# Pair-wise half transposes, narrower tables, two tokens a row and spread tail stores in an attention and mixer kernel

## The chip, the cores and the metric

The kernel runs on one core of one Trainium2 chip. The metric is the device time of one execution in microseconds (us). The profile's "span" runs from the first to the last instruction of one profiled execution and is some 1.7 us shorter than the time of the same run. Each run has a state: "slow" when it is over 1.5% above the fastest run of the same kernel. Ratios use fast runs only. The medians in the tables include slow runs. Engines: PE is the matrix engine (PEld its weight loads), DVE is VectorE, ACT is ScalarE, POOL is GpSimd, SP is the engine whose queue issues the DMAs.

## The reference, cut to what matters

```python
# q, k, v: (8, 8, 576, 64); window 128, ALiBi slopes 2**-(h+1)
scores = q @ k.T / 8 + bias            # only 0 <= row - column < 128
x      = softmax(scores) @ v           # -> (8, 576, 512)
W_tok  = (x @ w_q) @ (x @ w_k).T / 8   # the token mixer, no softmax
out    = relu(W_tok @ x) @ w_out       # float32
```

## The kernel before

The kernel builds a list of operations for 8 batches (loads, casts, transposes of q and k, scores S, exponentials E, bias products M, value products PV, normalisations N, transposes of x, the mixer products WK, WQ, G, MX, the relus R, output products O, tail outputs OT, stores). A fixed string, PLAN, gives each operation its place in the order, its engine and its PSUM bank; every engine works through its part in that order. These are the parts that the change touches:

```python
# tables exp(-slope * distance), 1024 columns a head, all written by ACT
nc.scalar.activation(out=table[:, h, :].rearrange("p (a b) -> p a b", a=4),
    in_=rel.unsqueeze(1).broadcast_to([P, 4, 256]), func=AF.Exp, scale=s)
nc.scalar.activation(out=table[:, h, 960:1024], in_=rel[:, 0:64], func=AF.Exp, scale=s)
...
# x transposed one pair of heads (c) at a time, five 128x128 blocks, one bank
for t in range(5):
    nc.tensor.transpose(bank(bk[0]).bitcast(F16)[:, P * t : P * t + P],
                        xs[b % 2][:, t, P * c : P * c + P], ident)
copy(eng, xT[b % 2][:, c, 0:S], bank(bk[0]).bitcast(F16)[:, 0:S])
...
# outputs: 128 tokens a block, two blocks in one store, the 64 tail tokens of two batches in another
nc.tensor.matmul(bank(bk[0]), rm[:, b % 2, db, P * t : P * t + P], wout_sb[:, db, :], ...)
nc.sync.dma_start(out=out[b, P * (t - 1) : P * (t + 1), :].rearrange("(t p) d -> p t d", t=2), in_=osb[n % 3])
nc.sync.dma_start(out=out[2 * pr : 2 * pr + 2, 512:576, :], in_=osbt[pr % 2])
```

The first store writes 512 KB (there are 16 of them), the second 256 KB (4 of them, called tail stores below; the fourth belongs to the end of the kernel).

The softmax here doesn't subtract the row's maximum and nothing guards it: scores larger than these inputs give would overflow.

## Time and profile before

| | before |
|---|---|
| time, median of the first 3 runs (range) | 163.13 us (160.31 to 163.85) |
| span of the profiled run | 159.1 us |
| busy, whole span | PE 83%, DVE 76%, ACT 78%, POOL 39% |
| busy from 40 to 130 us | PE 95%, DVE 93%, ACT 90% |

The page of the kernel before, busy time by engine and its course in 40 slices of 4 us (9 is 90% or more):

```profile
PE 132.0 (83%) x2180; PEld 87.5 (55%) x2180; DVE 121.6 (76%) x200; ACT 123.5 (78%) x178; POOL 62.7 (39%) x82
...
PE   6446579649989999999999999999989699999700
...
DVE  4467468986999989999799897989899896643300
ACT  6999939684999799989979888999899642748300
...
PEclk9955558996999999999999999999999999999995
DMA  5999999999995899799999999989138973054570
```

Three engines are nearly full in the middle at once. The DMA row shows mostly full engines in the middle (with a 5 near 48 us and a 7 near 64 us). The deep hole is in the slices from 111 to 119 us (1 and 3), and at the end the row falls again. The same page's chain of waits, by engine:

```profile
PE 44%; ACT 23%; DVE 13%; DMA 5%; POOL 5%; issue 4%; POOLq 0%
```

The start, from the timeline of ACT (start us, length us, engine, line, operation, out<-in, count):

```profile
2.60 8.75 ACT L164 ACTIVATE table<-rel 128x1024 f16<-128x1024 f32 x14 [0.52 <-POOL rel L164]
11.26 2.83 ACT L164 ACTIVATE pt<-bank 128x1024 f16<-128x1024 f32 x3
13.97 1.35 ACT L164 ACTIVATE table<-rel 128x1024 f16<-128x1024 f32 x2
```

ACT writes tables without a gap until the first exponential (`pt<-bank`) at 11.26 us. The DMA queue in the middle, from the timeline of SP:

```profile
105.27 0.72 SPq L164 DMA_DIRECT2D out_dram<-osbt  x1
106.04 0.57 SPq L164 DMA_DIRECT2D ldv<-in_v_dram  x1
106.66 6.08 SPq L164 DMA_DIRECT2D out_dram<-osbt  x1
112.78 3.25 SPq L164 DMA_DIRECT2D ldv<-in_v_dram  x1
116.14 3.07 SPq L164 DMA_DIRECT2D out_dram<-osb  x1
```

Two tail stores are issued at 105.3 and 106.7 us; the second holds the queue for 6.08 us. What the tail stores do by themselves is seen in the trace's single DMA packets. Busy DMA engines, counted from the packets of the output stores (2 KB each):

```
 112.0 to 114.5 us   2.1 engines of 16, nothing else moves
 154.5 to 157.5 us   2.1 engines of 16, nothing else moves
```

The chain of waits in order of time shows the store that came after them:

```profile
116.14 8.34 DMA out_dram<-osb
...
124.50 0.59 ACT osb L164
```

And the end: timeline, then what the closing instructions on SP waited for:

```profile
147.36 0.52 SPq L164 DMA_DIRECT2D out_dram<-osbt  x1
...
150.28 0.58 ACT L164 COPY osb<-bank 128x512 f32<-128x512 f32 x1 [0.28 <-PE bank L164]
```

```profile
SPq L713 <- DMA out_dram<-osbt: 4.3, 1, 4.3
```

The last output copy ends at 150.86 us, 8.2 us before the end of the span; of these the kernel waits 4.3 us for the last tail store alone. The transposes of x, from the groups of instructions (busy us, mean ns):

```profile
L164 DVE COPY xT<-bank 128x576 f16<-128x576 f16 x32 | 13.2, 450 | 1.4 <-PE bank L164 1.1
L164 PE MATMUL bank<-ident,x 128*128 128x128 f16 x160 | 12.0, 220 | 0.1
```

### The profile page before, as it was taken

The page shows a single profiled execution, that of the slowest core. Times are in us where ns is not written, and L with a number is a line of the kernel's source. Part 1 is how long each engine was busy: PE and PEld are TensorE (multiplying, and loading weights), DVE is VectorE, ACT ScalarE, POOL GpSimd, SP SyncE. Part 2 cuts the span into 40 slices and gives each one's busy share as a digit, 9 for nine tenths or more (in the row PEclk, how much of TensorE's full clock was granted, in tenths as well). Part 3 has the DMA queues.
Part 4 walks back from the last instruction along what each step waited for, and adds up shares of the span by engine and source line. Part 5 has one row for each costly group of instructions (what it writes and reads, how often), then busy time and mean ns, then how long its engine had stood idle before and what let it go on. Part 6 is the DMA issues. An engine that isn't in the chain of part 4 may idle for free.

```text
span 159.1 us, 5064 instructions
## 1 busy us (share of the span) xinstructions
PE 132.0 (83%) x2180; PEld 87.5 (55%) x2180; DVE 121.6 (76%) x200; ACT 123.5 (78%) x178; POOL 62.7 (39%) x82
## 2 busy tenths in 40 slices
PE   6446579649989999999999999999989699999700
PEld 6334467538657566476665556576655457643200
DVE  4467468986999989999799897989899896643300
ACT  6999939684999799989979888999899642748300
POOL 4553542682664596465742445154530500000000
PEclk9955558996999999999999999999999999999995
DMA  5999999999995899799999999989138973054570
GB/s 167 370 227 334 220 380 189 336 313 314 261 291 215 270 329 280 241 262 334 348 352 272 282 297 335 311 229 215 59 106 230 298 303 140 13 165 158 158 268 35
DMA packets 52703, 39.39 MB, mean 248 GB/s; under 512 B 39368, under 2 KB 39368, under 8 KB 52680
## 3 DMA queue, kind: packets, MB, share of 16 engines
q1 hardware_dynamic: 52680, 39.07, 85.4%
q8 instruction: 17, 0.28, 0.8%
q14 instruction: 6, 0.05, 0.1%
HBM read 29.62 MB, written 9.44 MB: 246 GB/s over the span
## 4 chain that ended last, share of the span: by engine, by line
PE 44%; ACT 23%; DVE 13%; DMA 5%; POOL 5%; issue 4%; POOLq 0%
PE bank L164 44%; ACT pt L164 11%; ACT table L164 6%; DMA out_dram<-osb 5%; DVE pt L164 4%; DVE x L164 3%; POOL nat L164 3%; DVE qT L164 2%; ACT qT L164 2%; ACT kT L164 2%; ACT osb L164 1%; DVE xT L164 1%; DVE inv L164 1%; DVE wkn L164 1%; DVE wqT L164 1%
## 5 line engine op out<-in xcount | busy, mean ns | idle before, releaser
L164 ACT ACTIVATE pt<-bank 128x1024 f16<-128x1024 f32 x64 | 63.2, 1035 | 8.7 <-PE bank L164 8.6
L164 POOL CAST nat<-ld 128x1152 f16<-128x1152 f32 x32 | 36.4, 1149 | 25.0 <-DVE pt L164 12.2
L164 DVE TENSOR_TENSOR pt<-pt,table 128x2048 f16<-128x2048 f16 x32 | 39.6, 1245 | 0.3 <-ACT pt L164 0.2
L164 POOL CAST vt<-ldv 128x512 f16<-128x512 f32 (+1 forms) x37 | 22.5, 627 | 33.4 <-DVE pt L164 16.2
L164 PE MATMUL bank<-wout_sb,rm 128*128 128x512 f16 x128 | 31.7, 380 | 1.3 <-ACT osb L164 1.3
L164 PE MATMUL bank<-qT,kT 64*128 64x256 f16 (+2 forms) x320 | 25.7, 269 | 5.2 <-DVE qT L164 2.5
L164 DVE TENSOR_TENSOR x<-bank,inv 128x640 f16<-128x640 f32 x32 | 25.7, 816 | 0.7
L164 PE MATMUL bank<-vt,pt 128*128 128x65 f16 x576 | 24.0, 199 | 1.2 <-ACT kT L164 0.7
L164 PEld LDWEIGHTS <-pt 128*128 128x128 f16 x576 | 21.8, 101 | 5.5 <-issue 1.9
L164 PEld LDWEIGHTS <-kT 64*128 64x128 f16 x320 | 14.6, 100 | 14.1 <-issue 10.4
L164 PE MATMUL bank<-ident,nat 64*128 64x64 f16 x576 | 14.5, 198 | 7.4 <-POOL nat L164 4.1
L164 ACT COPY osb<-bank 128x512 f32<-128x512 f32 x22 | 13.0, 613 | 8.7 <-PE bank L164 7.1
L164 PEld LDWEIGHTS <-rm 128*128 128x128 f16 x128 | 11.0, 98 | 13.2 <-issue 2.4
L164 PEld LDWEIGHTS <-nat 64*128 64x128 f16 x576 | 12.0, 99 | 11.3 <-POOL nat L164 7.3
L164 ACT ACTIVATE rm<-bank 128x512 f16<-128x512 f32 x23 | 14.0, 607 | 2.5 <-PE bank L164 2.3
L164 DVE COPY xT<-bank 128x576 f16<-128x576 f16 x32 | 13.2, 450 | 1.4 <-PE bank L164 1.1
L164 ACT COPY kT<-bank 128x1152 f16<-128x1152 f16 x11 | 12.4, 1136 | 1.1 <-PE bank L164 1.1
L164 DVE COPY qT<-bank 128x1152 f16<-128x1152 f16 x7 | 9.4, 1355 | 4.4 <-PE bank L164 4.3
L164 PE MATMUL bank<-ident,x 128*128 128x128 f16 x160 | 12.0, 220 | 0.1
L164 ACT COPY qT<-bank 128x1152 f16<-128x1152 f16 x9 | 10.1, 1121 | 1.3 <-PE bank L164 1.2
L164 PEld LDWEIGHTS <-x 128*128 128x128 f16 x160 | 9.3, 97 | 2.7 <-issue 1.6
L164 DVE COPY osb<-bank 128x512 f32<-128x512 f32 x10 | 6.9, 687 | 4.9 <-PE bank L164 4.9
(42 smaller groups left out, 123.2 us busy)
## 6 DMA issues: line engine op xcount, KB each, us to landing
ld<-in_k_dram SPq DMA_DIRECT2D x16, 576.0 KB, 6.5
ld<-in_q_dram SPq DMA_DIRECT2D x16, 576.0 KB, 6.1
ldv<-in_v_dram SPq DMA_DIRECT2D x32, 256.0 KB, 7.4
out_dram<-osb SPq DMA_DIRECT2D x16, 512.0 KB, 4.9
ldv<-in_v_dram SPq DMA_DIRECT2D x8, 128.0 KB, 5.8
osb<-in_moe_w_out_dram SPq DMA_DIRECT2D x2, 512.0 KB, 6.2
out_dram<-osbt SPq DMA_DIRECT2D x4, 256.0 KB
osbt<-in_moe_w_k_dram SPq DMA_DIRECT2D x1, 128.0 KB, 6.2
```

The source lines that it names most:

```text
L164: r = call(*a, **k)
```

## The change

Its intent, part by part: transposes that use both partition halves of PE at once, for two pairs of heads together (less PE time); tables for which ACT computes 256 columns and DVE copies the rest (less ACT time); two consecutive tokens a partition, so that a row of 4 KB is contiguous in memory; tail stores whose slowest dimension is 64 rows and no longer 2 batches, so that all DMA engines take part. PLAN is new from end to end: the order, the engines and the banks. The diff, cut to its core:

```diff
-            nc.scalar.activation(
-                out=table[:, h, :].rearrange("p (a b) -> p a b", a=4),
-                in_=rel.unsqueeze(1).broadcast_to([P, 4, 256]), func=AF.Exp, scale=s)
-            nc.scalar.activation(out=table[:, h, 960:1024], in_=rel[:, 0:64], func=AF.Exp, scale=s)
+            nc.scalar.activation(out=table[:, h, 0:256], in_=rel, func=AF.Exp,
+                                 scale=-(2.0 ** (-(h + 1))))
+    for f in range(2):                                   # four heads each, on DVE
+            t = table[:, 4 * f : 4 * f + 4]
+            for a in range(1, 4):
+                w = 256 if a < 3 else 192
+                nc.vector.tensor_copy(out=t[:, :, 256 * a : 256 * a + w], in_=t[:, :, 0:w])
+            nc.vector.tensor_copy(out=t[:, :, 960:1024], in_=t[:, :, 0:64])
... (transposes of x, now for c - 1 and c together)
-                for t in range(5):
-                    nc.tensor.transpose(bank(bk[0]).bitcast(F16)[:, P * t : P * t + P],
-                                        xs[b % 2][:, t, P * c : P * c + P], ident)
+                for a in range(2):
+                    for t in range(5):
+                        for i in range(2 if t < 4 else 1):
+                            r = slice(64 * i, 64 * i + 64)
+                            o = bank(bk[i]).bitcast(F16)
+                            w = 64 * ((5 - i) * a + t)
+                            nc.tensor.transpose(o[:, w : w + 64],
+                                xs[b % 2][r, t, P * (c - 1 + a) : P * (c + a)], ident[r, r])
... (outputs)
-                    nc.tensor.matmul(bank(bk[0]), rm[:, b % 2, db, P * t : P * t + P],
+                    r = slice(256 * (t // 2) + t % 2, 256 * (t // 2) + 256, 2)
+                    nc.tensor.matmul(bank(bk[0]), rm[:, b % 2, db, r],
-    ....rearrange("(t p) d -> p t d", t=2)
+    ....rearrange("(p t) d -> p t d", t=2)
-                nc.sync.dma_start(out=out[2 * pr : 2 * pr + 2, 512:576, :], in_=osbt[pr % 2])
+                for i in range(2):
+                    nc.sync.dma_start(out=out[2 * pr + i, 512:576, :],
+                                      in_=osbt[pr % 2][64 * i : 64 * i + 64])
... (PLAN: every line is new)
```

In the new PLAN ACT takes the casts of the first k and q, which POOL had. And after the last value product nine output groups follow on PE, where eleven followed before.

More of the change, by code (lines that the diff above doesn't have):

```diff
@@ L30 @@
 FOREVER = 1000
-DENSE = (False, False)
 class Op:
@@ L102 @@
 PLAN = """
-1G 7D 37S 0G 2D 33S 4D 45S 3G 5D 12P0 41S 6D 13P0 24A 57S 9P0 53S 10P0 18A 49S 14P0 59S 20A 11P0
-63S 38G 15P0 55S 19A 8P0 51S 39P2 31S 34G 21A 40D2 29S 71S 35P0 17A 85S 36D0 46G 67S 22A 248P0
-47P2 42G 241P4 249A0 48D2 243P6 244A6 58G 43P0 44D0 246P2 242A4 54G 23A 245D 256P0 253P4 251P6
-247A2 50D 252A6 258P2 60G 254A4 61P6 62D6 257A0 64G 259A2 65P0 56D 16P4 66A0 250D 52A 255D 83S
-406P0 401P2 79S 30G 407D0 32G 263P4 77S 402D2 408D0 268P6 264A4 93S 403D2 89S 411P0 72G 269A6 81S
-261P4 412D0 409P2 262A4 75S 260D 73P6 97S 404P3 74A6 86G 27S 405D3 416P4 413D0 111S 266P6 417D4
@@ L109 @@
-68G 105S 87P0 267A6 418D4 101S 265D 69P4 115S 419P3 70A4 414P6 80G 410D2 420D3 84G 278P4 415D6
-276P2 279A4 270D 271P6 272A6 78G 563P4 94G 277A2 564D4 273P6 88D0 274A6 95P2 90G 96D2 91P0 82G
-561P2 92A0 562D2 76G 275D 107S 426P0 109S 286P2 421P4 98G 427D0 287A2 103S 428D0 281P6 25S 422D4
-282A6 283P2 423D4 119S 28G 431P0 123S 284A2 432D0 288P4 280D 99P6 100A6 565P2 112G 433D0 289A4
-436P6 566D2 106G 296P0 437D6 569P2 438D6 297A0 429P4 102G 424P5 430D4 573P6 570A2 285D 291P0 434P4
-574A6 439P2 292A0 116G 425D5 293P6 435D4 440D2 294A6 113P4 290D 117P0 567P2 118A0 575P6 108G 114D4
@@ L115 @@
-568A2 577P7 110G 104G 571P0 576D6 298P2 572A0 578D7 135S 446P4 295D 299A2 145S 441P0 149S 26G
-447D4 308P6 442D0 448D4 451P2 127S 309A6 443D0 120G 141S 301P4 129S 579P6 302A4 452D2 453D2 137S
-300D 131S 306P0 121P2 307A0 133S 303P4 678P7 136G 580D6 163S 122A2 124G 171S 456P0 444P6 304A4
-457D0 449P2 146G 445D6 675P3 458D0 679A7 581P4 450D2 676A3 147P6 150G 582D4 454P0 148A6 459P1
-455D0 125P2 151P4 128G 460D1 126A2 583P6 310D 589P0 152A4 313P2 142G 584D6 591P1 314A2 590D0 587P4
-318P6 588D4 130G 319A6 673P0 305D 161S 316P2 159S 585P4 317A2 593P6 138G 674D0 155S 592D1 586A4
@@ L121 @@
-153S 143P2 320D 594A6 167S 311P0 680P4 312A0 189S 132G 144D2 677S 597P6 681A4 134G 139P0 157S
-140A0 315D 466P4 175S 461P2 193S 598A6 164G 467D4 693P0 468D4 462D2 323P6 694A0 463D2 471P4 172G
-324A6 321P0 472D4 473D4 476P2 322A0 162G 333P6 477D2 338P4 478D2 334A6 160G 469P0 464P1 470D0
-336P2 339A4 325D 331P6 474P0 332A6 479P4 156G 465D1 683P5 475D0 337A2 154G 187S 480D4 328P0 682S
-165P6 173P2 166A6 185S 685P4 174D2 168G 181S 329A0 605P6 686D4 684A5 326P2 606D6 601P0 190G 327A2
-603P4 687S 602D0 183S 599P6 191P2 330D 201S 169P0 192A2 688P5 179S 600D6 197S 170A0 158G 604D4
@@ L127 @@
-689D5 205S 481P2 207S 343P0 482D2 483D2 486P4 176G 344A0 348P6 487D4 346P2 349A6 335D 607P0 347A2
-194G 488D4 595P6 608A0 341P2 177P4 350D 596A6 491P0 342A2 696P6 340D 178A4 698P7 186G 492D0 493D0
-697A6 690P2 188G 699A7 182G 351P0 691D2 613P4 484P3 614A4 496P6 692S 485D3 352A0 703P2 700S 497D6
-498D6 223S 609P4 358P0 345D 219S 610A4 611P6 701P3 612A6 184G 359A0 494P4 702D3 499P5 202G 195P6
-495D4 489P3 196A6 500D5 615P0 490D3 356P4 180G 704D2 616A0 617P3 211S 357A4 506P0 209S 618D3 501P6
-198G 507D0 213S 353P2 502D6 508D0 215S 716P4 354A2 227S 206G 503D6 361P0 717A4 199P2 355D 203P6
@@ L133 @@
-362A0 621P4 204D6 208G 200A2 239S 366P0 708P5 367A0 622D4 718S 360D 233S 363P2 709A5 368P0 695S
-364A2 511P6 231S 504P4 512D6 711P5 369A0 513D6 224G 516P2 505D4 712A5 376P0 517D2 371P4 518D2
-377A0 619P6 220G 372A4 373P2 620D6 225P0 370D 519P6 374A2 509P7 514P4 706P5 212G 520D6 226A0 510D7
-210G 515D4 221P2 629P6 707A5 375D 627P0 631P4 222A2 710S 713P5 214G 235S 632D4 628A0 630D6 216G
-237S 526P2 714A5 705S 378P0 527D2 528D2 217P4 379A0 715S 633P6 228G 218A4 635P7 634D6 365D 229P0
-636A7 623P2 388P4 230D0 240G 624A2 521P6 234G 389A4 531P2 522D6 637P0 532D2 523D6 386P4 638A0
@@ L139 @@
-533D2 387A4 625P6 232G 381P0 626D6 643P2 382A0 393P4 380D 383P6 394A4 524P0 726P1 644D2 384A6 236G
-525D0 639P4 391P2 390D 640A4 536P6 392A2 724P0 238G 537D6 538D6 727A1 396P4 398P2 395D 397A4 641P6
-719P1 642A6 385D 529P4 539P5 725A0 534P6 399A2 721P7 728S 540D5 530D4 739P0 720A1 535D6 400D 722A7
-541P2 723S 546P4 542D2 543D2 729P1 547D4 731P2 548D4 556P6 732A2 645P3 730A1 557D6 551P4 733S
-646D3 647P1 552D4 553D4 649P2 558D6 544P3 648D1 650A2 549P4 545D3 740A0 559P5 554P1 560D5 741S
-657P2 653P6 550D4 658A2 734P0 555D1 654A6 736P1 735A0 659P0 737D1 655P2 660D0 651P4 738S 656A2
@@ L145 @@
-661P1 652A4 663P0 662D1 742P1 664D0 744P0 743A1 671P2 745A0 669P4 667P6 672D2 747P1 668A6 746S
-670A4 665P2 748D1 749P0 666A2 762P1 750A0 751S 754P0 763A1 764S 752P1 755D0 753D1 757P0 756S 759P1
-758A0 760A1 761S
+1G 6D 39S 4D 0G 35S 2D 7D 47S 3G 8P0 5D 43S 14P0 20A 65S 19A 11P0 23A 59S 18A 12P0 17A 61S 24A 25D
+21A 9P0 57S 22A 40A 15P0 53S 26D 13P0 51S 10P0 55S 36A 41P2 73S 42D2 69S 37P0 31S 38A0 48G 33S
+250P0 99S 49P2 251A0 44G 245P4 91S 50D2 243P6 77S 244A6 45P0 248P2 66G 46D0 246A4 249A2 67P6 247D
@@ new lines @@
+260P0 255P4 261A0 258P2 62G 68D6 60A 253P0 259A2 58D 63P6 252D 64A6 256A4 262D 254A0 52D 54D 56A
+257D 85S 403P0 95S 406P2 79S 404D0 74G 405D0 265P4 81S 263P6 266A4 407D2 83S 408D2 411P0 70G 87S
+264A6 414P4 412D0 413D0 117S 75P2 32G 71P6 29S 415D4 34G 409P0 416D4 72A6 27S 410D0 113S 417P4
+76A2 268P6 100G 418D4 270P0 269A6 280P2 267D 101P4 281A2 273P6 92G 102D4 274A6 531P2 78G 271A0
+532D2 278P6 93P4 86G 275P2 279A6 272D 535P0 94A4 96G 533P1 536D0 276A2 534D1 80G 537P4 539P0 277D
+111S 97P2 538A4 16P6 125S 98A2 82G 540D0 109S 84G 105S 282D 103S 427P0 419P2 107S 88G 428D0 121S
@@ new lines @@
+295P4 420D2 429D0 422P6 296A4 143S 421D2 293P0 118G 89P4 294A0 423D6 424D6 430P2 90A4 431D2 30G
+541P0 425P6 432D2 542A0 283P4 426D6 433P2 284A4 28G 288P0 434D2 285P6 286A6 297D 290P4 547P2 289A0
+543P6 287D 545P3 544A6 300P0 114G 546D3 291A4 119P6 548D2 549P3 120D6 301A0 126G 298P4 550A3 115P0
+292D 127P6 299A4 650P2 110G 128D6 116A0 645P3 106G 651A2 112G 137S 557P0 646D3 553P4 104G 643P2
+139S 554A4 558D0 133S 108G 644A2 135S 302D 435P0 131S 438P2 129S 122G 436D0 310P4 439D2 440D2
+648P6 147S 311A4 647S 437D0 303P2 144G 649A6 123P4 304A2 124D4 138G 145P0 446P6 146A0 308P2 140G
@@ new lines @@
+447D6 448D6 443P4 309A2 555P0 444D4 441P6 134G 445D4 556A0 141P2 142A2 442D6 449P0 305P4 136G
+450D0 306A4 551P6 313P2 552D6 559P0 314A2 132G 307D 315P4 163S 318P6 316A4 320P2 157S 655P1 130G
+560D0 151S 319A6 451P4 159S 321A2 663P0 148G 195S 452D4 453D4 177S 323P6 664A0 312D 325P2 165S
+149P4 656A1 161S 563P0 324A6 322D 169S 326A2 561P1 155S 317D 652S 454P6 564A0 462P2 150A4 164G
+455D6 562D1 653P0 463D2 152G 456D6 459P4 654A0 464D2 660P1 160G 657S 460D4 158G 461D4 173S 153P2
+661A1 328P6 189S 154D2 658P0 329A6 196G 203S 330P4 191S 659D0 565P6 333P2 331A4 199S 566D6 178G
@@ new lines @@
+457P0 334A2 465P4 458D0 197P6 466D4 198A6 338P0 166G 571P2 572D2 340P4 339A0 573P6 327D 341A4
+575P7 162G 574D6 335P0 569P2 567P4 336A0 170G 577P6 568D4 570A2 576D7 156G 179P0 578D6 167P2 180A0
+171P4 332D 467P6 168A2 666P0 337D 172A4 668P1 468D6 469D6 470P2 667A0 669A1 579P4 471D2 581P6
+472D2 174G 580A4 673P0 670S 582A6 662S 585P2 342D 175P4 185S 586A2 345P6 671P1 346A6 183S 190G
+674D0 181S 478P2 204G 176A4 672D1 187S 348P6 479D2 207S 480D2 475P0 349A6 192G 350P4 476D0 583P2
+477D0 351A4 473P6 200G 474D6 481P0 584A2 343P4 482D0 344A4 353P6 355P2 352D 587P0 356A2 683P1
@@ new lines @@
+588D0 354A6 347D 678P0 684A1 186G 193P2 679A0 358P4 194D2 360P6 359A4 591P0 184G 361A6 357D 215S
+201P2 205P4 209S 202A2 589P1 182G 592D0 221S 681P6 590D1 206A4 217S 188G 211S 362D 491P0 682A6
+233S 483P2 225S 492D0 486P4 484D2 216G 493D0 676P6 208G 487D4 485D2 686P7 210G 677A6 488D4 680S
+597P0 687A7 370P2 598D0 213S 494P4 371A2 222G 675S 593P6 495D4 373P0 594A6 496D4 241S 489P2 374A0
+229S 380P6 490D2 218G 497P4 665S 498D4 381A6 223P2 375P0 212G 224D2 365P4 237S 376A0 601P6 235S
+366A4 603P7 602D6 685S 377D 363P0 239S 599P2 368P4 364A0 605P6 600D2 226G 369A4 604D7 595P0 606D6
@@ new lines @@
+234G 227P2 596A0 219P4 372D 378P6 220A4 696P0 214G 228D2 379A6 694P1 697A0 367D 613P4 607P2 609P6
+608A2 689P0 610A6 382D 507P2 614A4 691P6 690A0 242G 508D2 509D2 695A1 499P4 230G 692A6 611P0 500D4
+383P2 501D4 612A0 693S 502P6 384A2 688S 238G 231P0 503D6 504D6 510P4 232A0 698S 709P2 236G 511D4
+512D4 385P0 505P6 386A0 400P4 506D6 701P3 401A4 710D2 240G 398P0 702D3 513P6 711S 399A0 393P4
+514D6 699P2 394A4 402D 615P3 700A2 395P0 616D3 388P4 703S 396A0 390P6 387D 617P2 389A4 619P3 618D2
+397D 391A6 515P0 706P2 620A3 516D0 392D 621P4 625P6 622A4 704P3 517D0 707A2 626D6 518P4 705A3
@@ L148 @@
+627P0 519D4 708S 523P6 520D4 628A0 623P2 524D6 526P0 624A2 525D6 521P4 527D0 528D0 714P2 522D4
+529P0 715A2 712P3 530D0 629P2 713D3 631P0 630D2 716S 633P1 632D0 717P0 634A1 639P2 637P4 635P6
+640A2 638D4 641P2 636D6 719P1 642A2 718D0 727P2 720D1 729P3 728A2 721S 724P2 730A3 731S 722P3
+725A2 732P2 723A3 726S 733A2 734S
 """
@@ L348, in steps, with f_exps, f_table @@
     for h in range(H):
-        def f_table(eng, bk, h=h):
-            s = -(2.0 ** (-(h + 1)))
-            nc.scalar.activation(
-                out=table[:, h, :].rearrange("p (a b) -> p a b", a=4),
-                in_=rel.unsqueeze(1).broadcast_to([P, 4, 256]), func=AF.Exp, scale=s)
-            nc.scalar.activation(out=table[:, h, 960:1024], in_=rel[:, 0:64], func=AF.Exp,
-                                 scale=s)
-        op({"ACT": 1.2}, f"table{h}", -20 + (h // 4 * 2 + h % 2) * SLOT, f_table, reads=[("mask", 0)],
-           writes=[("table", h)])
+        def f_exps(eng, bk, h=h):
+            nc.scalar.activation(out=table[:, h, 0:256], in_=rel, func=AF.Exp,
+                                 scale=-(2.0 ** (-(h + 1))))
+        op({"ACT": 0.29}, f"exps{h}", -30 + h, f_exps, reads=[("mask", 0)], writes=[("exps", h)])
+    for f in range(2):
+        def f_table(eng, bk, f=f):
+            t = table[:, 4 * f : 4 * f + 4]
[3 more added lines that the diff above has]
+            nc.vector.tensor_copy(out=t[:, :, 960:1024], in_=t[:, :, 0:64])
+        op({"DVE": 1.15}, f"table{f}", -20 + 2 * f * SLOT, f_table,
+           reads=[("exps", 4 * f + h) for h in range(4)], writes=[("table", f)])
     def f_ldw(eng, bk, i):
@@ L404, in f_xpose @@
                             o = bank(bk[a]).bitcast(F16)
-                            o = o[:, j:S:9] if DENSE[x] else o[:, 64 * j : 64 * j + 64]
-                            nc.tensor.transpose(o, n[r, j].rearrange("p i d -> p (i d)"),
+                            nc.tensor.transpose(o[:, 64 * j : 64 * j + 64],
+                                                n[r, j].rearrange("p i d -> p (i d)"),
                                                 ident[r, r])
@@ L411, in f_evac @@
                     src = pairs[bk[0] // 2].bitcast(F16).rearrange("p (a w) -> p a w", a=2)[:, :, 0:S]
-                    if not DENSE[x]:
-                        dst = dst.rearrange("p a (g j) -> p a g j", j=9)
-                        src = src.rearrange("p a (j g) -> p a g j", j=9)
-                    copy(eng, dst, src)
+                    copy(eng, dst.rearrange("p a (g j) -> p a g j", j=9),
+                         src.rearrange("p a (j g) -> p a g j", j=9))
                 name = f"{'qk'[x]}{b}{f}"
-                op({"SP": 0.6}, "ld " + name, base - 14, f_load, writes=[("ld", i)], dma=1.75)
+                op({"SP": 0.6}, "ld " + name, base - 14, f_load, writes=[("ld", i)], dma=1.65)
                 op({"POOL": 1.12} if b else {"POOL": 1.12, "DVE": 1.15, "ACT": 1.0},
@@ L422, in steps @@
                    opens=(key, 2), mode="R")
-                op({"ACT": 1.0, "DVE": 0.85 if DENSE[x] else 1.26}, "evac " + name, base - 3.5,
+                op({"ACT": 1.0, "DVE": 1.26}, "evac " + name, base - 3.5,
                    f_evac, psum=key, reads=[("kzero", 0)] * x, writes=[(("qT", "kT")[x], 2 * b + f)])
@@ L438, in steps @@
             op({"SP": 0.6}, f"ld v{b}{kb}", base - 12, f_loadv, writes=[("ldv", i)],
-               dma=1.4 if kb < 4 else 0.7)
+               dma=1.33 if kb < 4 else 0.67)
             op({"POOL": 0.6} if b else {"POOL": 0.6, "DVE": 0.6, "ACT": 0.5}, f"cast v{b}{kb}",
@@ L479, in steps @@
             op({"DVE": 1.15}, f"M{b}{c}", base + 1.5, f_bias,
-               reads=[("P", n), ("table", h0), ("table", h0 + 2)], writes=[("PM", n)])
+               reads=[("P", n), ("table", c // 2)], writes=[("PM", n)])
     for b in range(NB):
@@ L521, in steps @@
                writes=[("x", n)])
+            if c % 2 == 0:
+                continue
             def f_xt(eng, bk, b=b, c=c):
-                for t in range(5):
-                    nc.tensor.transpose(bank(bk[0]).bitcast(F16)[:, P * t : P * t + P],
-                                        xs[b % 2][:, t, P * c : P * c + P], ident)
-            def f_xte(eng, bk, b=b, c=c):
-                copy(eng, xT[b % 2][:, c, 0:S], bank(bk[0]).bitcast(F16)[:, 0:S])
+                for a in range(2):
[4 more added lines that the diff above has]
+                            w = 64 * ((5 - i) * a + t)
+                            nc.tensor.transpose(
+                                o[:, w : w + 64],
+                                xs[b % 2][r, t, P * (c - 1 + a) : P * (c + a)], ident[r, r])
+            def f_xte(eng, bk, b=b, c=c):
+                dst = xT[b % 2][:, c - 1 : c + 1, :].rearrange("p a (t i w) -> p a t i w", t=5, i=2)
+                for i in range(2):
+                    n = 5 - i
+                    copy(eng, dst[:, :, 0:n, i], bank(bk[i]).bitcast(F16)[:, 0 : 128 * n].rearrange(
+                        "p (a t w) -> p a t w", a=2, t=n))
             key = f"XT{b}{c}"
-            op({"PE": 0.28}, key, prio + 1.6, f_xt, reads=[("x", n - c % 2), ("x", n - c % 2 + 1), ("ident", 0)],
-               opens=(key, 1))
-            op({"DVE": 0.38}, f"XTe{b}{c}", prio + 2.0, f_xte, psum=key,
-               reads=[("zero", 0)], writes=[("xT", n)])
+            op({"PE": 0.28}, key, prio + 1.6, f_xt,
+               reads=[("x", n - 1), ("x", n), ("ident", 0)], opens=(key, 2), mode="R")
+            op({"DVE": 0.74}, f"XTe{b}{c}", prio + 2.0, f_xte, psum=key,
+               reads=[("zero", 0)], writes=[("xT", n - 1), ("xT", n)])
     for b in range(NB):
@@ L628, in f_store @@
                     nc.sync.dma_start(
-                        out=out[b, P * (t - 1) : P * (t + 1), :].rearrange("(t p) d -> p t d", t=2),
+                        out=out[b, P * (t - 1) : P * (t + 1), :].rearrange("(p t) d -> p t d", t=2),
                         in_=osb[n % 3])
-                op({"SP": 0.6}, f"st{b}{t}", base + t * SLOT + 1.6, f_store, dma=1.5,
+                op({"SP": 0.6}, f"st{b}{t}", base + t * SLOT + 1.6, f_store, dma=1.45,
                    reads=[("osb", n)])
@@ L644, in f_storet @@
             def f_storet(eng, bk, pr=pr):
-                nc.sync.dma_start(out=out[2 * pr : 2 * pr + 2, 512:576, :], in_=osbt[pr % 2])
+                for i in range(2):
+                    nc.sync.dma_start(out=out[2 * pr + i, 512:576, :],
+                                      in_=osbt[pr % 2][64 * i : 64 * i + 64])
             key = f"OT{pr}"
@@ L651, in steps @@
                writes=[("osbt", pr)])
-            op({"SP": 0.6}, f"stt{pr}", base + SLOT + 1.5, f_storet, dma=0.75, reads=[("osbt", pr)])
+            op({"SP": 1.15}, f"stt{pr}", base + SLOT + 1.5, f_storet, dma=0.75, reads=[("osbt", pr)])
     return ops
```

## The prediction

> **What bounds it now.** The span is 159.1 us. From 40 to 130 us the windows view has PE 96%, DVE 93% and ACT 90% busy: three nearly full engines, so relieving one gains little alone. Before 40 us PE is half idle. The chain of waits is PE 44%, ACT 23% (6% writing the table), DVE 13%. Three places stand out in the timeline:
> - Start: ACT writes tables from 2.6 to 11.35 us (1045 and 256 ns each) and again at 14.0. The first exponential starts at 11.26 us; its scores were ready near 9.7.
> - Middle: tail stores (256 KB each) are issued at 105.3 and 106.7 us. The packets show about 2 DMA engines busy from 111 to 116.5 and 118 to 119.5 us (1 and 3 tenths in the page's DMA row). The second issue holds the SP queue 6.1 us; an output store issued at 116.1 takes 8.3 us and stands on the chain (5%); v casts wait up to 5.5 us for loads.
> - End: the last output copy ends at 150.9 us, normal stores finish near 154.2, but the last tail store trickles on 2 engines to 157.9.
>
> The Trainium skill, "DMA: Bandwidth & Descriptors", section "Why a DMA increments its semaphore by 16 and not by 1", says that the slowest dimension decides how many engines a DMA uses; here it is 2, and the trace agrees (2.1 engines busy, 2 KB packets of 84 ns).
>
> **What the change does.**
> - Tail stores as two 64-row DMAs: an estimate of 0.75 us on 16 engines instead of 5.4 on 2. The end gains about 3 us, all critical. The hole of 6 to 8 us goes; as PE had other work, I count 1.5 us.
> - Tables: ACT loses 10.4 us and gets eight exponentials of 256 columns (estimate 2.5 us in all) and two early casts. DVE gets two sets of copies, an estimate of 1.2 us each, near 4 to 7 us, where it idled. First exponential near 9 us. But the first value product needs v, whose loads (the same bytes) land near 19 us, so I expect 2 to 3 us to survive.
> - x transposes: ten 128x128 per pair take about 0.65 us of PE (20 took 1.29); eighteen on 64-row halves should take 0.32, as in the q/k transposes (18 weight loads in 0.32). That is 0.3 us x 16 = 5 us of PE, partly visible, as DVE is as full. DVE evacuation stays equal (2 x 0.39 us now).
> - Two tokens a row: 4 KB packets; 84 ns per 2 KB is already the engine's rate, so nothing. Stride-2 weight loads hide behind 512-column matmuls.
> - The whole plan is reordered: DVE gets about +4 us in all, ACT -6, POOL -4. After the last value product nine output groups follow instead of eleven, 1.8 us of PE.
>
> **Sum.** 3 (end) + 2.5 (start) + 1.5 (hole) + 2 (transposes, shorter tail), less 0.5 for DVE: 8.5 us, so 154.5 us, range 150 to 159.5. Faster by over 2%: 0.89; within: 0.09; slower: 0.02.
>
> **What would show it.** No stretch with 2 DMA engines; end of PE to end of span 5 to 6 us (now 8.9); first exponential at 9 us; x transposes 0.4 us a pair; DVE busy near 125 us.
>
> **What would make it wrong.** The strided xT evacuation running at 1 column per ns (+0.5 us x 16 on DVE, which is full); pair banks making PE wait more; a start wholly load-bound.

## The result, and the profile after

| | before | after |
|---|---|---|
| time, median | 161.81 us (4 runs, 160.31 to 163.85) | 150.36 us (4 runs, 149.59 to 151.41) |
| span of the profiled run | 159.1 us | 149.7 us |

The ratio is 0.938, 95% interval 0.931 to 0.946. A ratio is the mean time of one kernel's fast runs over that of the other's of the same rounds, so it is not the ratio of the medians above (two of the four runs of before are slow). The two fast runs of before have a mean of 160.4 us. Measured again later, on another occasion with more runs, it was 0.933 (0.928 to 0.938). 1% of the time before is 1.6 us. The page of the kernel after:

```profile
PE 125.7 (84%) x2308; PEld 82.6 (55%) x2308; DVE 125.7 (84%) x212; ACT 118.5 (79%) x170; POOL 58.9 (39%) x78
...
PE   6567388676889979889989999999789999999870
...
DVE  5749987979999998789999989999799989994700
ACT  6959937995889868997799999959889989741560
...
PEclk9999999999999999999999999999999999999999
DMA  4999999999999999999999999799699896033075
```

The work moved as intended: PE has 6.3 us less, ACT 5.0 less, DVE 4.1 more, POOL 3.8 less. The hole in the DMA row is gone. The clock row's nines at the start are not a better clock: the clock records of this run begin at 24 us, and before that a group of q/k transposes took 0.66 us, as in the half-clock stretch of before, against 0.44 at full clock. The chain of waits, by engine:

```profile
PE 40%; DMA 16%; DVE 13%; ACT 12%; SPq 9%; POOL 4%; issue 2%; POOLq 0%; DVEq 0%
```

DMA and the SP queue rose from 5% to 25% of it (16% and 9%): the loads, and the queue that issues them, now stand on the chain in stretches. The start, on ACT's timeline:

```profile
2.63 2.56 ACT L159 ACTIVATE table<-rel 128x256 f16<-128x256 f32 x8 [0.55 <-POOL rel L159]
5.09 2.19 ACT L159 CAST nat<-ld 128x1152 f16<-128x1152 f32 x2
...
9.86 1.02 ACT L159 ACTIVATE pt<-bank 128x1024 f16<-128x1024 f32 x1 [0.70 <-PE bank L159]
```

The first exponential comes 1.4 us earlier, at 9.86 us. The end (timeline, then the wait of the closing instructions), and the transposes (groups):

```profile
145.09 0.58 ACT L159 COPY osbt<-bank 128x512 f32<-128x512 f32 x1 [0.28 <-PE bank L159]
145.70 1.11 SPq L159 DMA_DIRECT2D out_dram<-osbt  x2
```

```profile
SPq L726 <- DMA out_dram<-osbt: 1.8, 1, 1.8
```

```profile
L159 DVE COPY xT<-bank 128x640 f16<-128x640 f16 x16 | 7.7, 482 | 0.4 <-PE bank L159 0.4
...
L159 PE MATMUL bank<-ident,x 64*128 64x64 f16 x288 | 7.3, 190 | 0.9 <-DVE x L159 0.7 <-DVE osb L159 0.2
...
L159 DVE COPY xT<-bank 128x512 f16<-128x512 f16 x16 | 6.6, 415 | 0.0
```

The last copy ends at 145.67 us, 4.0 us before the end instead of 8.2. A pair's evacuation on DVE costs 482 + 415 = 897 ns, as before (2 x 450). So where did the 9.4 us of span go? Two instructions that exist in every variant cut the run into three stretches: the end of the last normalisation N of batch 7 (the last attention work on DVE), and the end of the last output copy. The same cut for variants of the experiments:

| us | to the last N | then to the last output copy | then to the end of the span |
|---|---|---|---|
| before | 135.2 | 15.7 | 8.2 |
| after | 133.4 | 12.3 | 4.0 |
| b_tail | 135.3 | 15.7 | 4.0 |
| a_all | 139.4 | 12.5 | 9.2 |
| a_table | 137.1 | 12.3 | 4.0 |

After against before: -1.8, -3.4 and -4.2 us. Less than a fifth of the gain lies in the 133 us before the last normalisation. This is one execution of each kernel, and the one of after was the slowest of its four fast runs (151.41 us, median 150.36), so the first stretch is uncertain by some 1 us.

### The profile page after: what moved, and what is told of

It is laid out like the page before. It is cut to its first block, busy times and chain, and to the rows that moved or that the text cites. A ratio compares the mean times of both kernels' runs of the same rounds, so it can differ in the third digit from the quotient of the medians.

```text
span 149.7 us, 5314 instructions
## 1 busy us (share of the span) xinstructions
PE 125.7 (84%) x2308; PEld 82.6 (55%) x2308; DVE 125.7 (84%) x212; ACT 118.5 (79%) x170; POOL 58.9 (39%) x78
## 4 chain that ended last, share of the span: by engine, by line
PE 40%; DMA 16%; DVE 13%; ACT 12%; SPq 9%; POOL 4%; issue 2%; POOLq 0%; DVEq 0%
PE bank L159 40%; DMA ld<-in_q_dram 10%; SPq L159 9%; ACT pt L159 8%; DMA ld<-in_k_dram 6%; DVE pt L159 5%; POOL nat L159 2%; ACT qT L159 2%; DVE xT L159 2%; POOL vt L159 2%; DVE x L159 2%; ACT kT L159 1%; DVE kT L159 1%; DVE osb L159 1%; DVE rm L159 1%
## 5 line engine op out<-in xcount | busy, mean ns | idle before, releaser
L159 POOL CAST nat<-ld 128x1152 f16<-128x1152 f32 x30 | 34.2, 1146 | 36.7 <-PE bank L159 10.6
L159 DVE TENSOR_TENSOR pt<-pt,table 128x2048 f16<-128x2048 f16 x32 | 41.0, 1293 | 2.1 <-ACT pt L159 2.0
L159 POOL CAST vt<-ldv 128x512 f16<-128x512 f32 (+1 forms) x35 | 20.8, 613 | 25.4 <-DVE pt L159 15.5
L159 PEld LDWEIGHTS <-pt 128*128 128x128 f16 x576 | 21.4, 102 | 9.7 <-issue 2.6
L159 DVE TENSOR_TENSOR x<-bank,inv 128x640 f16<-128x640 f32 x32 | 25.8, 817 | 0.8
L159 PEld LDWEIGHTS <-nat 64*128 64x128 f16 x576 | 12.2, 100 | 10.1 <-POOL nat L159 4.7
L159 ACT COPY qT<-bank 128x1152 f16<-128x1152 f16 x12 | 13.5, 1121 | 2.6 <-PE bank L159 2.6
L159 DVE COPY kT<-bank 128x1152 f16<-128x1152 f16 x8 | 10.8, 1354 | 3.2 <-PE bank L159 3.2
L159 DVE COPY xT<-bank 128x640 f16<-128x640 f16 (+1 forms) x32 | 12.5, 448 | 0.4 <-PE bank L159 0.4
L159 PE MATMUL bank<-x,wkn 128*64 128x512 f16 x80 | 10.1, 383 | 0.0
L159 PE MATMUL bank<-wqT,gm 64*128 64x256 f16 x64 | 8.4, 288 | 1.5 <-DVE wqT L159 0.6
L159 ACT COPY kT<-bank 128x1152 f16<-128x1152 f16 x8 | 9.1, 1138 | 0.5 <-PE bank L159 0.5
L159 DVE TENSOR_SCALAR rm<-bank 128x512 f16<-128x512 f32 x11 | 7.5, 684 | 2.3 <-PE bank L159 2.2
```

Source lines behind the costliest of these rows:

```text
L159: r = call(*a, **k)
```

## The experiments

Names that begin with a_ are the kernel after with something undone, those with b_ the kernel before with something done. All gave correct results, all were timed against the kernel before in 5 rounds. Their ratios to before are compared. The profiles of a_tail, a_xt, a_last, a_rows, b_table, b_table3 and after_again fell in the slow state; of these, times are taken from the fast runs, and the profile only for busy sums, counts, single durations and the start of the run. (b_table3 is read up to 45 us; until then its clock records show the same stretches as those of before, within 0.4 us.)

### a_tail, a_xt, a_table, a_all: which part gains, in the new order

a_tail stores each tail with one DMA again (the diff's last hunk reversed). a_xt makes ten full transposes and two dense evacuations per pair:

```diff
+                for a in range(2):
+                    for t in range(5):
+                        nc.tensor.transpose(bank(bk[a]).bitcast(F16)[:, P * t : P * t + P],
+                                            xs[b % 2][:, t, P * (c - 1 + a) : P * (c + a)], ident)
...
+                for a in range(2):
+                    copy(eng, xT[b % 2][:, c - 1 + a, 0:S], bank(bk[a]).bitcast(F16)[:, 0:S])
```

a_table lets ACT write 1024 columns a head again and DVE copy only the last 64. a_all undoes these three and the row layout, so that only PLAN is new.

> The kernel after, with the tail store as one DMA of 2 x 64 rows again. Theory (the store's spread is worth its 3 us at the end, and the hole in the middle costs little because the engines have other work): ratio to the kernel before near 0.96 (after has 0.938), that is 3 to 4 us lost, nearly all of it after the last matmul. Rival (the hole also costs, because loads and stores wait behind two busy engines): 5 us or more lost, ratio 0.97 or above, and the last exponentials later than in after.

> The kernel after, with ten full 128x128 transposes and two dense 576-column evacuations per pair instead of eighteen half transposes; same plan. Theory (PE is bound, so 5 us less PE work are partly visible): 2 to 4 us lost, ratio 0.95 to 0.965. Rival (PE had slack where the transposes stand, loads bound the middle): under 1 us lost, ratio 0.938 to 0.945. PE busy time rises by about 5 us in either case.

> The kernel after, with ScalarE writing 1024 columns of every table again and VectorE copying only the last 64. Theory of the prediction (2.5 us of the saved start survive): ratio near 0.955. Rival (what the start gains is given back by about 30 us, because loads decide when the work can go on; the last exponentials of after end at 127.6 us, as before at 128.0): under 1 us lost, ratio at most 0.945, although the first exponential comes some 6 us later.

> All four parts undone in the order of the kernel after: old tail store, old transposes, old tables, old row layout; only the order of instructions and the choice of engines is new. If the new order is what gains beside the store: ratio 0.96 to 0.975, so about half of the gain of after is left. If the parts gain and the order does not: ratio 0.99 or above.

| | ratio to before | 95% interval |
|---|---|---|
| after (both measurements) | 0.938, 0.933 | 0.931 to 0.946, 0.928 to 0.938 |
| a_tail | 0.971 | 0.966 to 0.977 |
| a_xt | 0.949 | 0.944 to 0.955 |
| a_table | 0.959 | 0.954 to 0.963 |
| a_all | 1.010 | 1.004 to 1.015 |

The rival "the new order is what gains by itself" falls: the order alone is 1% slower than before. Whether the parts need the new order is a different question. For the tail stores and the tables it is taken up below; the transposes, and all parts together, were not run in the old order. Against the two values of after, the tail stores are worth 3.3 to 3.8% (5.3 to 6.2 us), more than the theory's 3 to 4 us and in the rival's range (where they are worth it is the next question), the transposes 1.1 to 1.6% (1.7 to 2.6 us, the interval of a_xt just reaches that of the first measurement of after), the tables 2.0 to 2.6% (3.3 to 4.1 us). The worth of the transposes reaches the lower end of the theory's 2 to 4 us and lies above the rival's 1 us. In a_xt PE is busy 131.5 us instead of 125.7, but the transposes of x account for 4.0 of these 5.8 us only (11.3 against 7.3 in the groups of instructions; the profile is a slow one), so of 4.0 us PE time some four to six tenths were visible. The three-stretch table shows what the order does: a_all reaches the last normalisation 4.2 us later than before, then needs 3.2 us less to the last copy, since fewer output groups are left, and then 1.0 us more, since its last instruction is the slow tail store. So nearly all of the 3.4 us between the last normalisation and the last copy is the order's. The order moves output work forward; the parts pay for that.

Why a_table is so late is seen on its ACT timeline:

```profile
2.63 7.68 ACT L159 ACTIVATE table<-rel 128x1024 f16<-128x1024 f32 x8 [0.55 <-POOL rel L159]
10.21 2.19 ACT L159 CAST nat<-ld 128x1152 f16<-128x1152 f32 x2
...
14.98 1.02 ACT L159 ACTIVATE pt<-bank 128x1024 f16<-128x1024 f32 x1 [0.70 <-PE bank L159]
```

In the new order the first two casts stand behind the tables on ACT. Long tables delay the very first transposes, and the first exponential comes at 14.98 us, 5.1 us later than in after and 3.7 later than in before. So this run overstates what tables are worth by themselves; they had to be tried in the old order.

### a_last, b_tail: the end of the run or the hole in the middle

a_last spreads only the fourth tail store, b_tail is the kernel before with all four spread and nothing else:

```diff
 # a_last
+                if pr < 3:
+                    nc.sync.dma_start(out=out[2 * pr : 2 * pr + 2, 512:576, :], in_=osbt[pr % 2])
+                    return
 # b_tail
-                nc.sync.dma_start(out=out[2 * pr : 2 * pr + 2, 512:576, :], in_=osbt[pr % 2])
+                for i in range(2):
+                    nc.sync.dma_start(out=out[2 * pr + i, 512:576, :],
+                                      in_=osbt[pr % 2][64 * i : 64 * i + 64])
```

> The kernel after, with only the last of the four tail stores spread; the first three again run on two engines in mid-kernel. Undoing all four cost 0.033 of the time before (0.971 against 0.938), some 5 us. Theory (prediction): 3 to 3.5 us of that are the end, so this run loses 1.5 to 2 us against after, ratio 0.947 to 0.952. Rival 1 (the hole is free, all is the end): ratio at most 0.941. Rival 2 (the hole is the larger part): ratio 0.958 or above.

> The kernel before with nothing changed but the spread tail stores, in its own order of instructions. If the part is worth the same in either order: ratio 0.965 to 0.972 (about 5 us). If the old order hides more of it (the long hole at 111 to 119 us stood in this order): a larger gain, 0.955 or below; if it hides all but the end: 0.978 to 0.982.

b_tail: 0.972 (0.967 to 0.977), 2.8% or some 4.5 us. Its profile answers the question of the middle: the last normalisation ends at 135.3 us (before 135.2), the last copy at 151.0 (150.9), the span at 155.0 (159.1). All of the gain lies after the last copy. The page's DMA row has no hole near 111 to 119 us any more, the last copy stands where it stood, and the wait for the tail store is gone from the closing instructions (page, timeline, waits):

```profile
DMA  4999999999999299999999799999999507333384
```

```profile
150.39 0.59 ACT L164 COPY osb<-bank 128x512 f32<-128x512 f32 x1 [0.28 <-PE bank L164]
```

```profile
SPq L715 <- DMA out_dram<-osb: 2.5, 1, 2.5
```

The 8 us hole of the DMA engines, which had looked so bad, was free in this order. (The ratio lies in the range that I had given for "worth the same in either order"; for the end alone I had expected 0.978 to 0.982, so I had made the end too small.) a_last: 0.944 (0.938 to 0.951), between the ranges of the theory and of the first rival, 0.6 to 1.1% above after, so three slow stores in the middle of the new order cost 1.0 to 1.8 us, if anything; the intervals overlap with that of after's first measurement. The difference between a_tail and a_last, 2.7%, is again the end, about 4.3 us.

### a_rows: two tokens a row

```diff
-                    r = slice(256 * (t // 2) + t % 2, 256 * (t // 2) + 256, 2)
-                    nc.tensor.matmul(bank(bk[0]), rm[:, b % 2, db, r],
+                    nc.tensor.matmul(bank(bk[0]), rm[:, b % 2, db, P * t : P * t + P],
-    "(p t) d -> p t d"
+    "(t p) d -> p t d"
```

> The kernel after, with one token a row (2 KB packets, contiguous weight loads) again. Theory: within 0.5 us of after, ratio 0.935 to 0.942. Rival (the four parts undone together lost 1.2 us more than tail, transposes and tables one by one; that is the row layout): ratio 0.943 to 0.948.

0.9405 (0.935 to 0.946): nothing that these runs tell from after. A 2 KB packet takes 84 ns in the median (before), a 4 KB packet 159 ns (after), so the rate of one DMA engine rises from 24.4 to 25.8 KB/us only.

### b_table, b_table2, b_table3: the tables in the old order

b_table gives the kernel before the new table code: all eight exponentials first, the DVE copies (operations 765 and 766) before its first evacuation. POOL keeps the casts.

```diff
 # the body of the tables as in the diff of the change; in PLAN:
-24A .. 18A .. 20A .. 19A .. 21A 40D2 .. 17A .. 22A .. 23A
+24A .. 18A .. 20A .. 19A .. 21A 17A 22A 23A 765D 766D 40D2
```

> The kernel before with nothing changed but the tables: ScalarE writes 256 columns of each, VectorE copies the rest before its first evacuation. In the order of after this was worth about 3.3 us (0.959 against 0.938). If it is the freed ScalarE time and not the order that counts: ratio 0.978 to 0.985. If this order, which waits for v and other engines at 20 us anyway, gives the start back: ratio 0.99 or above.

1.004 (0.995 to 1.013): no gain, and the first exponential came at 12.88 us, later than in before. But this was a faulty test. The timeline of b_table, and then that of after:

```profile
4.58 5.08 DVE L120 COPY table<-table 128x1024 f16<-128x1024 f16 x8 [1.07 <-ACT table L120]
4.59 2.71 POOL L120 CAST nat<-ld 128x1152 f16<-128x1152 f32 x2 [2.02 <-DMA ld<-in_k_dram]
...
9.58 1.34 DVE L120 COPY kT<-bank 128x1152 f16<-128x1152 f16 x1
```

```profile
4.30 2.24 DVE L159 COPY table<-table 128x1024 f16<-128x1024 f16 x8 [0.88 <-ACT table L159]
6.99 1.36 DVE L159 COPY kT<-bank 128x1152 f16<-128x1152 f16 x1 [0.44 <-PE bank L159]
7.97 1.14 POOL L159 CAST nat<-ld 128x1152 f16<-128x1152 f32 x1 [5.38 <-DMA ld<-in_k_dram]
```

Beside POOL's casts the same eight copies take 5.08 us instead of 2.24. In the single instructions, a 1024-column copy that starts at 4.93 us, while a cast runs until 6.01, ends at 6.29 and takes 1364 ns instead of 423. The Trainium skill, "SBUF — State Buffer", section "Who interferes with whom", says that DVE and GpSimd share one port pair as an exclusive lock, so that the one that comes second blocks fully. The trace fits that: the copy ends 0.28 us after the cast, the next one 0.21 us after the next cast, and the first cast, which started together with a copy, took 1421 ns instead of 1147. (0.28 us is less than the 423 ns of a free copy, so part of its work must have been done before or during the wait.) In after, ACT has these casts; b_table2 below shows that this move is what lets the copies run free.

So b_table2 and b_table3 also move the two casts (38 and 34) to ACT.

```diff
 # b_table3, PLAN
-24A .. 18A .. 20A .. 38G .. 19A .. 39P2 .. 34G 21A 40D2 .. 17A .. 22A .. 23A
+24A 18A 20A 19A 21A 17A 22A 23A 765D 766D .. 38A .. 39P2 .. 34A 40D2
```

> As b_table, but ScalarE also takes the first two casts, as in after. In b_table the VectorE table copies ran beside GpSimd casts and took 5.1 us in all instead of 2.2 in after (one of 1024 columns 1364 ns instead of 423), which delayed the first evacuation to 9.6 us. If that collision ate the gain: copies back near 2.2 us, first exponential near 10 us, ratio 0.98 to 0.99. If this order gives the start back in any case, because the first value product waits for v near 20 us: ratio 0.995 or above.

> b_table2 once more, mended: there the first transpose had slipped ahead of the warm-up matmuls, so that 2.7 us of these stood before the second transpose and the first exponential came at 12.3 us. Now warm-ups come first, as in the kernel before; tables, copies and the two casts on ScalarE as in after. First exponential near 9.8 us (before 11.3). If the freed 8 us of ScalarE are worth something in this order: ratio 0.975 to 0.99. If this order gives the start back at the first value product (v near 20 us, then PE): ratio 0.993 to 1.003, and the first batch's last exponential under 1 us earlier than in before (19.9).

b_table2: 1.003 (0.999 to 1.008). The copies are back at 2.24 us, but my edit had put a transpose ahead of 24 warm-up matmuls, and the first exponential came at 12.29 us; a second faulty test. b_table3, mended: 0.998 (0.994 to 1.003). The first exponential now comes at 10.06 us, 1.2 us before that of the kernel before, and the gain then melts: the first batch's last exponential ends at 19.3 us (19.9), its last normalisation at 28.8 (29.1), the second batch's at 44.9 (44.9). In the old order the whole table part, with the casts moved, shows no gain (the interval leaves room for 0.6%). What the freed ACT time meets is in the chain of waits of b_table3:

```profile
2.31 8.37 DMA ld<-in_q_dram
...
10.73 1.16 POOL nat L120
...
15.54 3.77 ACT pt L120 x4
```

The fourth load lands at 10.67 us in before and in b_table3 alike, whatever ACT does. In b_table3 the fifth exponential waits for scores that follow from it, ACT stands idle for 1.3 us, and it starts at 15.54 us, only 0.6 us earlier than in before (16.14). After the last exponential ACT still has the next batch's evacuation of kT (to 20.3 us) and the last cast of v (to 20.8; before 21.4), and the first value products stand behind these: their first matmuls start at 20.95 us in before and 20.38 in b_table3, and all but three of them wait for that cast. So 0.6 us of the 1.2 are left there, and none at 44.9 us. In after the loads are ordered differently too: the fourth, issued at the same 2.3 us, lands at 9.42, no evacuation stands between the last exponential and the value products, and these start at 19.43. Which of these differences lets the new order use the tables was not tested one by one.

### a_actq, after_again: stores off the load queue

The chain of after holds 9% SP queue, so one more idea was to issue all output stores from ACT's queue, with no load behind them (with the stores' places in PLAN moved from S to A, and three lines of the kernel's dependency helper adapted to DMAs on ACT).

```diff
-                    nc.sync.dma_start(out=out[...
+                    nc.scalar.dma_start(out=out[...
```

> The kernel after with all output stores issued from ScalarE's queue, so that no load on the SP queue stands behind a store that waits for its copy (4.2 us at 80 us in after). If such loads are what holds the middle back: 1 to 3 us faster than after, ratio 0.92 to 0.932. If the DMA engines themselves are full: within 1 us of after. If issuing 24 stores costs ScalarE more than it frees (0.4 us each or more): slower than after by 1 us or more.

> The kernel after unchanged, on the same chip and in the same rounds, as the measure for a_actq and for the ratios of the earlier calls: 0.93 to 0.945.

after_again: 0.933. a_actq: 0.9875 (0.983 to 0.993), 5.4 points slower than after. One issue takes 0.34 us on ACT in the median, and about 0.5 us for a tail store; the 24 of them add up to 10.1 us in the trace, on an engine that was nearly full. ACT's idle time before exponentials grew from 9.3 to 13.4 us, and the page's DMA row now has a hole near 95 to 103 us:

```profile
DMA  4999999999999699899999994299999454033075
```

The idea failed. Whether the issue time alone did it, or the waits that ACT now has between its copies and the stores, these runs do not tell. No variant beat the kernel after.

## Why the prediction was right or wrong

The number was right: 154.5 us with a range of 150 to 159.5, measured 150.36; a gain of 8.5 us was forecast, and some 10 us came. The forecast is the sum taken off the median of 163.13 us, in which two of three runs were slow; off the 160.4 us of the fast runs it would have been 151.9. So of the 4.1 us between forecast and result 2.7 come from the base. And the total is partly luck: one term was worth nothing in the old order, others were too small, and they made up for each other. (One reading was off by a little: PE is busy 85.56 of the 90 us from 40 to 130, 95% and not 96%.) The terms of the sum, as the prediction put them:

- **"3 (end)"**: right in mechanism, too small. b_tail shows it alone: 8.2 us from the last copy to the end become 4.0, so 4.2 us. I had expected 5 to 6 us from the end of PE to the end; it is 4.6 (145.1 to 149.7).
- **"1.5 (hole)"**: wrong in the old order, where it is 0 (135.2 and 135.3 us to the last normalisation). The prediction said itself that PE had other work, and still counted 1.5 us. In the new order 1.0 to 1.8 us, not clear of noise.
- **"2.5 (start)"**: the step that failed, as a worth of the tables by themselves. It read "ACT loses 10.4 us" and "I expect 2 to 3 us to survive". Taken alone in the old order, with the casts on ACT, nothing survives (0.998). In the new order undoing the tables costs 3.3 to 4.1 us; this counts the casts that the order puts behind them, which no run took apart. Between before and after, the first value product starts 1.5 us earlier. The caution in the prediction was right for the old order: the first value product did wait for v there, but for its last cast on ACT (21.4 us) and not for its last load (19.25). The part and the order belong together: order alone +1.0%, tables alone -0.2%.
- **"2 (transposes, shorter tail)"**: too small. The stretch after the last normalisation is 3.4 us shorter (15.7 to 12.3). The transposes took 0.45 us a pair, near the forecast ("0.4 us a pair"; the sum had used 0.32), and a_xt puts them at 1.7 to 2.6 us in all. The shorter tail is nearly all the order's (a_all has 3.2 of the 3.4 us): it brings fewer output groups at the end, at a price of 4.2 us before (a_all), and the cheaper transposes help to pay it.
- **"less 0.5 for DVE"**: DVE has 125.7 us busy, forecast "near 125". Its cost was not isolated.
- **"Two tokens a row ... so nothing"**: agrees with a_rows. The stride-2 weight loads hid as forecast: a load takes 98 ns in after and 97 in a_rows, a matmul beside it 380 in both. **The strided evacuation** stayed equal (897 against 900 ns; the "2 x 0.39 us" of the prediction was too small already for before), so the first thing that could have made the prediction wrong did not happen.

Adding the parts: tail stores 3.3 to 3.8%, transposes 1.1 to 1.6%, and tables with the order about 1.0 to 1.6% (tables 2.0 to 2.6% less 1.0% for the order), give 5.4 to 7.0%; measured 6.2 and 6.7%.

## What to carry to other kernels

Look at the last microseconds first: a store that trickles on two engines cost nothing that could be seen in mid-kernel (old order) and 4.2 us at the end, because nothing runs beside it there. Busy time taken from a full engine is worth something only where the order of work can use it: the same tables gained nothing in the old order, and undoing them in the new one cost 2.0 to 2.6%, so test a part in both orders before you name its worth. And an experiment that moves work to another engine must be read instruction by instruction, since a copy beside a GpSimd cast took three times as long.

## What the Trainium skill lacked or had wrong

- "DMA: Bandwidth & Descriptors", section "Why a DMA increments its semaphore by 16 and not by 1": its rule for the number of engines held (2.1 of 16 busy for a slowest dimension of 2). I found no figure there for what such a DMA does to those behind it on the same queue: a 512 KB store issued after two of them took 8.3 us to land, against a median of 4.9. The runs do not settle it either: a store with none in front took 7.5 us, and one in after 8.7.
- "TensorE: Matmul & The Clock Gate", section "Part 4: PE-mode transpose": gives 390 ns for a 128x128 transpose in isolation and about 275 in a kernel. Back to back the trace has 20 of them in 1.29 us, 64 ns each, and 18 of half the rows on both halves in 0.45 us. The section lacks these rates, and by its latencies the gain of the half transposes can't be costed.
- No page that I read warns that a profile whose clock records begin late shows a mean granted clock of 1.0: here they begin at 24 us, while transposes before that took 0.66 us instead of 0.44.
- "SBUF — State Buffer", section "Who interferes with whom": right, and I had not used it; 423 ns became 1364 beside a GpSimd cast, and the cast's 1147 became 1421.
